# Column-halved products of key features and values in a linear-attention and feed-forward kernel

## The chip, the cores and the metric

The kernel runs on one core of one Trainium2 chip. The metric is the device time of one execution in microseconds. Before the change it is 1050.52 us, the median of three runs (1049.79 to 1050.94).

## What is computed

Attention with random features, and behind it a feed-forward layer with a gate of its own:

```
scale = 1 / sqrt(sqrt(D))                       # D = 64
def phi(x):                                     # omega: 128 features x 64
    proj = einsum('bhsd,md->bhsm', x, omega)
    h = proj - sum(x * x, axis=-1) / 2
    return exp(h - max(h, axis=-1)) / sqrt(128)
q_p, k_p = phi(q * scale), phi(k * scale)
kv  = einsum('bhsm,bhsd->bhmd', k_p, v)         # keys times values
z   = sum(k_p, axis=2)
num = einsum('bhsm,bhmd->bhsd', q_p, kv)
den = einsum('bhsm,bhm->bhs', q_p, z) + 1e-6
x   = (num / den) as 4608 tokens x 512
h   = x @ w_in                                  # 512 -> 2048
g   = h * erf(softplus(h))
out = g @ w_out                                 # 2048 -> 512
```

There are 8 batches of 8 heads, 576 positions each. Everything is in 32-bit floating point.

## The kernel before

**Tiles and stages.** Two heads make a pair: 1152 positions, cut into nine chunks of 128. There are 32 pairs. The first four are handled one by one (`first`), the others two at a time (`attention`, a quad). For each pair the key projection (`ppk`) goes through a maximum on VectorE and an exponential on ScalarE to the key features `fk`. Keys times values (`kvp`) sums over the positions: the stationary operand is a chunk of `fk`, 128 positions by 128 features, and the moving operand are the values `v`, 64 columns and a column of ones, which makes `z`. The fifth chunk holds the end of one head and the start of the other, so it is multiplied with two blocks of values at once, 130 columns, and the remaining eight with 65. VectorE or ScalarE copies `kvp` out of PSUM (`kh`, and from the thirteenth pair on a remainder `kl`). The query features are projected likewise (`ppq`), turned by transposes (`pt`), and multiplied with `kh` (`nd`); after a division they are the input `x` of the feed-forward layer. Its first product is `h`, `hS` or `hA` in the profile, its second `o`.

**The projections of a quad** (`project`, L999) put one pair's 64 dimensions in the upper and the other's in the lower 64 rows of TensorE's array, so that two products with half the rows run in one array. This is an arrangement that stands in the kernel before already.

**The order of the work.** No engine's order is written out by hand. `build` lists operations with the engines that can run them, an estimated cost (`COST`, L59) and a due time (`plan`); `Plan.order` (L135) runs through simulated time and gives each engine, when it is free, the ready operation that is due first. On TensorE it keeps account of the array's division: an operation named `proj...` has `half` set (L106), a change of `half` costs `COST["turnout"] / 2` (L246), and as long as the array is divided, another projection that is ready and due within `NEAR` = 6 us is taken ahead of a whole-array operation (L236). The order that comes out is the program order of each engine. TensorE works through it in order: a product that waits holds up all products behind it.

**What the change touches.** `key_values` of the emitter (L1017) issues `kvp` in two operations, `j` = 0 with five chunks and `j` = 1 with four; `key_values` of `build` (L575) registers them with a cost of 0.222 us a chunk and due times 0.08 of a quad's length apart, so other work can come between. `attention` (L679) calls it for both pairs of a quad, with due times 0.15 and 0.2.

The lines of the profile are those of a helper through which all instructions go (L858), so its groups are told apart by the names of the tiles.

Of the kernel before, what the change touches and what calls it, by code (L numbers as in the profile page):

```python
# [19 lines left out]
P = 128  # L20
B, H, S, D = 8, 8, 576, 64
NP = H // 2
S2 = 2 * S
NC = S2 // P
MID = NC // 2
D1 = D + 1
DM, DF = 512, 2048
T = 288
# [27 lines left out]
            ("S4", "B22", (((0, 1), (0, 1)),)))  # L56


COST = dict(mm=0.132, proj=0.224, turnout=0.40, tr=0.109, kv=0.222, table=1.3)  # L59
LAG = {"T": 0.35, "A": 0.35, "V": 0.33, "G": 0.33, "S": 0.3}  # L60
SLOTS = dict(w=8, u=2, un=2, f=2, mx=2, sq=2, v=2, qh=1, ql=1, kh=1, kl=1, rc=2, xs=4, xh=2, xl=2, u2=2,
             hs=4, gs=2, gh=6, gl=6, os=4, ps=8)
# [27 lines left out]
class Plan:  # L90
# [10 lines left out]
    def op(self, name, opts, fn, reads=(), writes=(), plan=None, set=None, macro=None, size=0,  # L101
           after=()):
        o = Op()
        o.opts, o.fn, o.plan, o.name, o.set, o.macro, o.size = opts, fn, plan, name, set, macro, size
        o.id = len(self.ops)
        o.half = name.startswith("proj")  # L106
        deps = {}
        uses = {}
        for a in after:
            deps[a.id] = a  # L110
        for t, key in reads:
            uses[t] = 1
            assert key in t.wr, (name, t.name, key)
            deps[t.wr[key].id] = t.wr[key]
            t.rd.setdefault(key, []).append(o)
        for t, key in writes:
            uses[t] = 1
            if key in t.wr:
                deps[t.wr[key].id] = t.wr[key]
            for r in t.rd.get(key, ()):  # L120
                if r is not o:
                    deps[r.id] = r
            t.wr[key], t.rd[key] = o, []
        o.alloc = []
        for t in uses:
            if not t.users:
                o.alloc.append(t)
                self.streams.setdefault(t.stream, []).append(t)
            t.users.append(o)
        o.uses = list(uses)  # L130
        o.deps = list(deps.values())
        self.ops.append(o)
        return o

    def order(self, slots, caps):  # L135
# [28 lines left out]
        ready = {e: [] for e in engines}  # L164
# [2 lines left out]
        until = {e: 0.0 for e in engines}  # L167
        events, out = [], []
        now, table, lock, bw = 0.0, "exp", None, 0.0
        port, piece, late, half = 0.0, 1.0, 0.0, False  # L170
        count = 0

        def push(o):
# [29 lines left out]
        while True:  # L203
            progress = True
            while progress:
                progress = False
                for e in engines:
                    if not idle[e]:
                        continue
                    skipped, chosen = [], None  # L210
                    while ready[e]:
                        item = heapq.heappop(ready[e])
                        o = item[2]
                        if o.start is not None:
                            continue
                        ok = can(o)
                        if ok and e == "A":
                            if lock is not None and o.set is not None and o.macro != lock:
                                ok = False
                        if ok:  # L220
                            slack = next(s for x, _, s in o.opts if x == e)
                            if e == "S":
                                ok = o.due - now < slack
                            elif o.due - now + late < slack and slack > -1e8:
                                ok = False
                        if ok:
                            chosen = o
                            break
                        skipped.append(item)
                        if len(skipped) > 500:  # L230
                            break
                    for item in skipped:
                        heapq.heappush(ready[e], item)
                    if chosen is None:
                        continue
                    if e == "T" and half and not chosen.half:  # L236
                        near = [x for x in ready[e] if x[2].half and x[2].start is None
                                and x[0] < now + NEAR and can(x[2])]
                        if near:
                            heapq.heappush(ready[e], (chosen.due, chosen.id, chosen))  # L240
                            chosen = min(near)[2]
                    o = chosen
                    progress = True
                    dur = next(c for x, c, _ in o.opts if x == e)
                    if e == "T":
                        if o.half != half:  # L246
                            dur += COST["turnout"] / 2
                        half = o.half
                        late += 0.1 * (max(0.0, now - o.due) - late)
                    if e == "V" and o.name in SHARED:  # L250

                        dur += max(0.0, until["G"] - now) % piece
                        port = now + dur
                    elif e == "G":
                        dur += max(0.0, port - now)
                        piece = dur / PIECES.get(o.name, 1) + 1e-6
                    o.eng, o.start = e, now
                    for t in o.alloc:
                        t.slot = free[t.pool].pop(0)
                        held[t.stream] += 1  # L260
                        nxt[t.stream] += 1
                    idle[e] = False
                    if e == "A":
                        if o.set is not None and o.set != table:
                            dur += COST["table"]
                            if o.set == "exp":
                                out.append("table")
                            table = o.set
                        if o.macro is not None:
                            lock = o.macro  # L270
                            if o.name.startswith("erf!"):
                                lock = None
                    out.append(o)
                    if e == "S":
                        event(now + 0.5, "idle", e)
                        begin = max(now, bw)
                        bw = begin + o.size / 300e3
                        o.end = bw + 2.0
                    else:
                        o.end = until[e] = now + dur  # L280
                        event(o.end, "idle", e)
                    busy[e] += dur
                    event(o.end, "done", o)
# [54 lines left out]
GATES0 = 10.0  # L338
RESTS0 = 15.0
SQA = 4.0  # L340
NEAR = 6.0
GROUPS = ((0, 3), (3, 6), (6, 9))
WHG = 5.0
WBG = -1e9
# [2 lines left out]
def build(emit):  # L347

    pl = Plan()
    E = emit  # L350
# [17 lines left out]
    def when(n, x):  # L368
        return pair_time(n, x) if n < NP else quad_time(n // 2, x)
# [207 lines left out]
    def key_values(n, t0):  # L577
        a = pairs[n]
        f, v = a["fk"], a["v"]
        kvp = a["kvp"] = pl.tile("ps", "kvp" + a["nm"], [P, 512], F32, "att", early(n))  # L580
        for j in range(2):
            pl.op("kv", [("T", (5 - j) * COST["kv"], -1e9)], lambda e, j=j: E.key_values(kvp, f, v, j),
                  reads=[(f, c) for c in range(NC)] + [(v, 0)], writes=[(kvp, 0)],
                  plan=when(n, t0 + 0.08 * j))
        whole = n < WHOLE
        kh = a["kh"] = pl.tile("kh", "kh" + a["nm"], [P, 2, P], F32 if whole else F32R)
        kl = a["kl"] = kh if whole else pl.tile("kl", "kl" + a["nm"], [P, 2, P], F32R)
        pl.op("kvhigh", [("V", 0.4, -1e9), ("A", 0.4, -1e9)], lambda e: E.kv_high(e, kh, kvp),
              reads=[(kvp, 0)], writes=[(kh, 0)])
        if not whole:  # L590
            pl.op("kvrest", [("V", 0.4, -1e9)], lambda e: E.kv_rest(kl, kvp, kh),
                  reads=[(kvp, 0), (kh, 0)], writes=[(kl, 0)])
# [86 lines left out]
    def attention(m):  # L679
# [2 lines left out]
        project(m, "k", 0.0)  # L682
        load(m, "q")
        key_values(2 * m, 0.15)
        key_values(2 * m + 1, 0.2)
        project(m, "q", 0.3)
        if m + 1 < N // 2:
            load(m + 1, "k")
# [152 lines left out]
def tile_attention_moe(ctx: ExitStack, tc: tile.TileContext, qT, kT, qN, kN, vP, omT, w1, w2, out):  # L841
# [64 lines left out]
    class Emit:  # L906
# [107 lines left out]
            for f, c, m, pp, k in parts:  # L1014
                act.activation(f.ap[:, c, :], pp.ap[:, k * P:(k + 1) * P], AF.Exp, bias=m)

        def key_values(self, kvp, f, v, j):  # L1017

            k = kvp.ap[:, :2 * P].rearrange("p (j d) -> p j d", j=2)[:, :, :D1]
            if j == 0:  # L1020
                pe.matmul(k, lhsT=f.ap[:, MID, :],
                          rhs=v.ap[:, MID * D1:(MID + 2) * D1].rearrange("p (j d) -> p j d", j=2),
                          start=True, stop=False)
            for c in range(MID) if j == 0 else range(MID + 1, NC):
                pe.matmul(k[:, j, :], lhsT=f.ap[:, c, :], rhs=v.ap[:, (c + j) * D1:(c + j + 1) * D1],
                          start=False, stop=c == NC - 1)


        def kv_parts(self, kvp, dst):
# [163 lines left out]
```

## Time and profile before

| | |
|---|---|
| median of the runs | 1050.52 us |
| profiled execution: time | 1049.21 us |
| profiled execution: span from the first to the last instruction | 1047.3 us |
| granted TensorE clock, mean | 0.998 |
| busy: PE, DVE, ACT, POOL | 1033.3, 757.0, 678.3, 466.9 us |
| share of the chain that ended last: PE | 93% |
| first and last start of a `kvp` matmul | 11.4 and 856.8 us |

PE is TensorE's multiplication, PEld its weight loads, DVE is VectorE, ACT is ScalarE, POOL is GpSimd. A row of a group gives the line, the engine, the operation, output<-inputs, the part of the array (rows*columns), the shape, the count, then busy time and the mean duration of one in ns, and the idle time before it with what ended it. The duration of a matmul is its way through the array; matmuls follow each other in the array like a pipeline, so their cost is read from the distances of their starts. A row of the timeline gives the start, the duration of the run of instructions that it merges, and what they are. An instruction in 32 bits on both sides has two records in the trace.

### The profile page before, as it was taken

Reading aid. Unit: us, or ns where it says so; the run is one execution under the profiler, and the core shown is the slowest. Engines: PE = TensorE matmul, PEld = TensorE weight load, DVE = VectorE, ACT = ScalarE, POOL = GpSimd, SP = SyncE. Lnnn points to the kernel's source line nnn. Section 1 sums busy time; section 2 is a strip of 40 time slices with the busy share of each in tenths; the row PEclk is TensorE's granted clock in tenths of the full one; section 3 lists DMA queues with packets and bytes.
Section 4 is the critical chain, followed back from the end, with each engine's and each line's share of the span. In section 5 each row is a group of like instructions: output and inputs, shape, how many; then the busy total and the mean of one; then the engine's idle time right before and its main releaser. Section 6 shows DMA issues by size and latency. Waiting matters only on the chain.

```text
span 1047.3 us, 21906 instructions
## 1 busy us (share of the span) xinstructions
PE 1033.3 (99%) x8208; PEld 1006.1 (96%) x8208; DVE 757.0 (72%) x1521; ACT 678.3 (65%) x1282; POOL 466.9 (45%) x469
## 2 busy tenths in 40 slices
PE   8999999999999999999999999999999999999998
PEld 7889999999999999999999999999999999999998
DVE  5989999987787577775777767776678756755541
ACT  8869958777685775766667566776567666353330
POOL 5726638867673344623455232741328212433300
PEclk9999999999999999999999999999999999999999
DMA  8664879798767787667767776677866756668771
GB/s 246 238 233 174 287 248 338 266 338 304 246 210 268 264 278 230 232 235 266 245 229 252 262 256 204 227 267 262 269 207 219 246 164 229 224 222 269 269 235 47
DMA packets 80137, 254.11 MB, mean 243 GB/s; under 512 B 8992, under 2 KB 9504, under 8 KB 80032
## 3 DMA queue, kind: packets, MB, share of 16 engines
q1 hardware_dynamic: 80032, 252.71, 71.0%
q8 instruction: 66, 1.08, 0.4%
q14 instruction: 39, 0.32, 0.1%
HBM read 218.07 MB, written 34.60 MB: 241 GB/s over the span
## 4 chain that ended last, share of the span: by engine, by line
PE 93%; DVE 2%; POOL 1%; DMA 1%; ACT 1%; SPq 1%; issue 1%; DVEq 0%; ACTq 0%
PE o L858 39%; PE hS L858 15%; PE hA L858 11%; PE h L858 9%; PE kvp L858 6%; PE nd L858 5%; PE ppq L858 3%; PE ppk L858 3%; PE pt L858 3%; DVE pw L858 1%; SPq L858 1%; DMA uq<-qT 1%; POOL unk L858 1%; ACT rc L858 0%; DVE xs L858 0%
## 5 line engine op out<-in xcount | busy, mean ns | idle before, releaser
L858 PE MATMUL o<-gh,w 128*128 128x288 f32 x2048 | 453.9, 300 | 1.9 <-DMA w<-wdw 1.4
L858 PEld LDWEIGHTS o<-gh,w 128*128 128x128 f32 x2048 | 340.4, 188 | 8.2 <-issue 1.6
L858 PE MATMUL o<-gl,w 128*128 128x288 f32 x1024 | 301.9, 295 | 0.0
L858 POOL TENSOR_TENSOR hs<-gs,hs 128x576 f32<-128x576 f32 x70 | 109.4, 1587 | 197.1 <-ACT gs L858 128.5
L858 PEld LDWEIGHTS o<-gl,w 128*128 128x128 f32 x1024 | 192.9, 188 | 0.3
L858 PE MATMUL hS<-xh,wS 128*128 128x288 f32 x768 | 186.4, 298 | 0.2 <-ACT hs L858 0.2
L858 PE MATMUL hA<-xh,w 128*128 128x288 f32 x576 | 148.3, 298 | 0.0
L858 PEld LDWEIGHTS hS<-xh,wS 128*128 128x128 f32 x768 | 134.3, 188 | 0.4 <-ACT hs L858 0.4
L858 POOL TENSOR_TENSOR gl<-hs,gh 128x576 fp32r<-128x576 f32 x64 | 99.6, 1579 | 46.7 <-ACT gh L858 29.1
L858 PE MATMUL h<-xh,w 128*128 128x288 f32 x512 | 119.5, 309 | 0.0
L858 ACT ACT_TABLE_LOAD x92 | 118.0, 1283 | 2.3 <-PEq L1184 0.7
L858 PE MATMUL hS<-xl,wS 128*128 128x288 f32 x384 | 113.3, 295 | 0.0
L858 POOL TENSOR_TENSOR unq<-unq 128x288 f32<-128x288 f32 (+2 forms) x63 | 48.1, 765 | 134.6 <-ACT unq L858 128.4
L858 ACT ACTIVATE fk<-ppk,mxk 128x128 f32<-128x128 f32 x288 | 77.4, 416 | 44.2 <-DVE mxk L858 44.0
L858 PEld LDWEIGHTS hA<-xh,w 128*128 128x128 f32 x576 | 103.3, 188 | 0.0
L858 ACT ACTIVATE rc<-nd,eps 64x288 f32<-64x288 f32 x128 | 63.5, 496 | 58.9 <-PE nd L858 55.2
L858 PEld LDWEIGHTS h<-xh,w 128*128 128x128 f32 x512 | 86.5, 190 | 2.7 <-DVE os L858 0.3
L858 ACT ACTIVATE fq<-ppq,mxq 128x128 f32<-128x128 f32 x288 | 77.9, 388 | 14.0 <-DVE mxq L858 13.8
L858 ACT ACTIVATE gs<-hs 128x1152 f32<-128x1152 f32 x64 | 73.0, 1163 | 19.8 <-DVE hs L858 19.4
L858 PE MATMUL hA<-xl,w 128*128 128x288 f32 x288 | 85.1, 296 | 0.0
L858 PE MATMUL h<-xl,w 128*128 128x288 f32 x256 | 76.1, 297 | 0.4 <-POOL xl L858 0.3
L858 PEld LDWEIGHTS hS<-xl,wS 128*128 128x128 f32 x384 | 72.4, 188 | 0.0
(109 smaller groups left out, 2100.9 us busy)
## 6 DMA issues: line engine op xcount, KB each, us to landing
w<-wdw SPq DMA_DIRECT2D x176, 512.0 KB, 4.7
wS<-wdcS SPq DMA_DIRECT2D x96, 512.0 KB, 4.8
st<-w SPq DMA_DIRECT2D x32, 512.0 KB, 4.8
wdw<-w SPq DMA_DIRECT2D x32, 512.0 KB, 3.5
w<-wdw SPq DMA_DIRECT2D x48, 256.0 KB, 4.2
v<-vP SPq DMA_DIRECT2D x32, 325.0 KB, 3.4
out<-os SPq DMA_DIRECT2D x32, 288.0 KB, 4.1
wdcS<-cS SPq DMA_DIRECT2D x16, 512.0 KB, 5.4
```

Source lines behind the costliest of these rows:

```text
L858: return tc.keep_in_program_order(method(*args, **kwargs))
```

## The change

Each chunk's product is issued as two instructions: one with the features 0 to 63 as the stationary operand, with its result in partitions 0 to 63, and one with the features 64 to 127 and partitions 64 to 127. Each stands on all 128 rows and on 64 columns of the array. The moving operand is the same for both. The two operations of a pair become one, with a cost of 1.08 us. The planner knows three divisions of the array now (`half` = 0, 1 or 2), stays in the same division when something of it is near, and `NEAR` is 12 us instead of 6. The second pair of a quad is due at 0.15 as the first, instead of 0.2. What goes in and what comes out, and the sums over chunks, are as before.

```diff
-COST = dict(mm=0.132, proj=0.224, turnout=0.40, tr=0.109, kv=0.222, table=1.3)
+COST = dict(mm=0.132, proj=0.224, turnout=0.40, tr=0.109, kv=1.08, table=1.3)
...
-        o.half = name.startswith("proj")
+        o.half = {"proj": 1, "kv": 2}.get(name[:4], 0)
...
-                    if e == "T" and half and not chosen.half:
-                        near = [x for x in ready[e] if x[2].half and x[2].start is None
+                    if e == "T" and half and chosen.half != half:
+                        near = [x for x in ready[e] if x[2].half == half and x[2].start is None
                                 and x[0] < now + NEAR and can(x[2])]
...
-NEAR = 6.0
+NEAR = 12.0
+KV1 = 0.15
...
         kvp = a["kvp"] = pl.tile("ps", "kvp" + a["nm"], [P, 512], F32, "att", early(n))
-        for j in range(2):
-            pl.op("kv", [("T", (5 - j) * COST["kv"], -1e9)], lambda e, j=j: E.key_values(kvp, f, v, j),
-                  reads=[(f, c) for c in range(NC)] + [(v, 0)], writes=[(kvp, 0)],
-                  plan=when(n, t0 + 0.08 * j))
+        pl.op("kv", [("T", COST["kv"], -1e9)], lambda e: E.key_values(kvp, f, v),
+              reads=[(f, c) for c in range(NC)] + [(v, 0)], writes=[(kvp, 0)], plan=when(n, t0))
...
         key_values(2 * m, 0.15)
-        key_values(2 * m + 1, 0.2)
+        key_values(2 * m + 1, KV1)
...
-        def key_values(self, kvp, f, v, j):
+        def key_values(self, kvp, f, v):
 
             k = kvp.ap[:, :2 * P].rearrange("p (j d) -> p j d", j=2)[:, :, :D1]
-            if j == 0:
-                pe.matmul(k, lhsT=f.ap[:, MID, :],
+            sides = (slice(0, D), slice(D, P))
+            for m in sides:
+                pe.matmul(k[m], lhsT=f.ap[:, MID, m],
                           rhs=v.ap[:, MID * D1:(MID + 2) * D1].rearrange("p (j d) -> p j d", j=2),
                           start=True, stop=False)
-            for c in range(MID) if j == 0 else range(MID + 1, NC):
-                pe.matmul(k[:, j, :], lhsT=f.ap[:, c, :], rhs=v.ap[:, (c + j) * D1:(c + j + 1) * D1],
-                          start=False, stop=c == NC - 1)
+            for c in (*range(MID), *range(MID + 1, NC)):
+                j = int(c > MID)
+                for m in sides:
+                    pe.matmul(k[m, j, :], lhsT=f.ap[:, c, m],
+                              rhs=v.ap[:, (c + j) * D1:(c + j + 1) * D1],
+                              start=False, stop=c == NC - 1)
```

More of the change, by code (lines that the diff above doesn't have):

```diff
@@ L169, in order @@
         now, table, lock, bw = 0.0, "exp", None, 0.0
-        port, piece, late, half = 0.0, 1.0, 0.0, False
+        port, piece, late, half = 0.0, 1.0, 0.0, 0
         count = 0
```

## The prediction

> **What bounds the kernel now.** I read the page first: the busy table and the chain that ended last.
>
> ```profile
> span 1047.3 us, 21906 instructions
> PE 1033.3 (99%) x8208; PEld 1006.1 (96%) x8208; DVE 757.0 (72%) x1521; ACT 678.3 (65%) x1282; POOL 466.9 (45%) x469
> ...
> PE 93%; DVE 2%; POOL 1%; DMA 1%; ACT 1%; SPq 1%; issue 1%; DVEq 0%; ACTq 0%
> PE o L858 39%; PE hS L858 15%; PE hA L858 11%; PE h L858 9%; PE kvp L858 6%; PE nd L858 5%; PE ppq L858 3%; PE ppk L858 3%; PE pt L858 3%; DVE pw L858 1%; SPq L858 1%; DMA uq<-qT 1%; POOL unk L858 1%; ACT rc L858 0%; DVE xs L858 0%
> ```
>
> TensorE carries 93% of the chain, and the next engine is busy 72% of the span. A busy share can hide waiting, because the ends of matmuls are modelled, so I asked next for the waits of PE alone; the three longest and the one of this product:
>
> ```profile
> PE ppk L858 <- ACT uk L858: 5.1, 1, 5.1
> PE o L858 <- DMA w<-wdw: 1.4, 1, 1.4
> PE ppk L858 <- DVE xs L858: 0.9, 2, 0.7
> ...
> PE kvp L858 <- DVE xs L858: 0.5, 1, 0.5
> ```
>
> Of these one, 5.1 us, is the wait for the first input; the others are about a microsecond each. So the time is the sum of what TensorE does, and a microsecond taken from it is a microsecond of the kernel, as long as nobody else becomes late.
>
> The product that changes is `kvp`. In the groups by shape each of its matmuls has two records (288 instructions, 576 records), which I call passes:
>
> ```profile
> L858 PE MATMUL kvp<-v,fk 128*128 128x65 f32 x512 | 63.5, 269 | 0.0
> L858 PE MATMUL kvp<-v,fk 128*128 128x130 f32 x64 | 12.7, 279 | 0.5 <-DVE xs L858 0.5
> ```
>
> Here 269 ns is the time that one pass is in the array, not what it costs, since passes overlap. The cost is the distance from start to start, and the timeline gives it. First the ruler, then two pieces of `kvp`, the second with the wide middle chunk (130 columns) ahead of its 65-column ones:
>
> ```profile
> 290.13 0.29 PE L858 MATMUL o<-gl,w 128*128 128x288 f32 x1
> 290.26 0.43 PE L858 MATMUL o<-gh,w 128*128 128x288 f32 x2
> 290.53 0.29 PE L858 MATMUL o<-gl,w 128*128 128x288 f32 x1
> ...
> 294.33 0.29 PE L858 MATMUL o<-gh,w 128*128 128x288 f32 x1
> 294.46 1.00 PE L858 MATMUL kvp<-v,fk 128*128 128x65 f32 x8
> 295.27 0.38 PE L858 MATMUL o<-gh,w 128*128 128x288 f32 x1
> 295.49 0.29 PE L858 MATMUL o<-gl,w 128*128 128x288 f32 x1
> ```
>
> ```profile
> 284.44 0.29 PE L858 MATMUL h<-xh,w 128*128 128x288 f32 x1
> 284.57 1.22 PE L858 MATMUL kvp<-v,fk 128*128 128x130 f32 x10
> 285.60 0.38 PE L858 MATMUL h<-xh,w 128*128 128x288 f32 x1
> 285.82 0.30 PE L858 MATMUL h<-xl,w 128*128 128x288 f32 x1
> ```
>
> Three `o` matmuls take 0.40 us, 0.133 each. From the `o` before `kvp` to the second `o` behind it 1.16 us pass (294.33 to 295.49); less two `o` at 0.133 that is 0.89 us for 8 passes, **0.111 us a pass**. The other piece: 1.38 less 0.27, 1.11 us for 10 passes, again 0.111, although two of the ten stream twice the columns. So streaming 65 columns is not what a pass waits for: what all ten share is the load of 128x128 weights, and that sets the 0.111. A pair has 18 passes, 2.0 us; 32 pairs cost 64 us, which is the 6% in the chain.
>
> **The change, part by part.** *The product.* 18 passes of 128x128 become 36 of 128x64, half of them for the left and half for the right part. No row of before has a product on half the columns. The nearest is the projection, which already runs two products at once, on the upper and the lower 64 rows:
>
> ```profile
> 296.42 0.29 PE L858 MATMUL o<-gh,w 128*128 128x288 f32 x1
> 296.64 0.37 PE L858 MATMUL ppq<-wq,uq 64*128 64x128 f32 x1
> 296.65 0.37 PE L858 MATMUL ppq<-wk,uq 64*128 64x128 f32 x1
> 296.86 0.27 PE L858 MATMUL ppq<-wq,uq 64*128 64x128 f32 x1
> 296.86 0.27 PE L858 MATMUL ppq<-wk,uq 64*128 64x128 f32 x1
> ...
> 297.97 0.27 PE L858 MATMUL ppq<-wq,uq 64*128 64x128 f32 x1
> 297.98 0.27 PE L858 MATMUL ppq<-wk,uq 64*128 64x128 f32 x1
> 298.18 0.40 PE L858 MATMUL o<-gh,w 128*128 128x288 f32 x1
> 298.42 0.30 PE L858 MATMUL o<-gl,w 128*128 128x288 f32 x1
> ```
>
> ```profile
> 296.64 0.18 PEld L858 LDWEIGHTS ppq<-wq,uq 64*128 64x128 f32 x1 [0.16 <-issue]
> 296.65 0.18 PEld L858 LDWEIGHTS ppq<-wk,uq 64*128 64x128 f32 x1
> ```
>
> Two loads and two multiplications start within 0.01 us of each other, and ten pairs of passes take 1.11 us (296.86 to 297.97): two products for the price of one. Halving the rows did not shorten a pass, still 0.111. Halving the columns should: a load of 64 columns and a stream of 65 are both half of the 128 that set 0.111, so a left-and-right pair should cost 0.056 (estimate, half of 0.111), and the wide chunk, 130 columns streamed, 0.111. A pair of heads is then 2 x 0.111 + 16 x 0.056 = 1.12 us instead of 2.0: 0.89 saved, **x 32 = -28.4 us**. Bounds of a left-and-right pair: 0.05 if it beats the halving a little (-31 us), and 0.111 if the halves share one load path or a load of half the columns takes as long as a whole one (0 us). I take 0.056, by the projection's row.
>
> The Trainium skill (TensorE: Matmul & The Clock Gate, LDWEIGHTS) has a weight load cost its number of columns over 1.2 GHz, whatever the rows: 107 ns for 128 columns, beside the 0.111 here, and the projection's unshortened pass agrees. By it the load of a half is 53 ns, and the sum would gain 1.5 us more.
>
> *Turning the array over.* The projection's rows price a change between whole and divided array: from 296.42 to 298.42 are 2.00 us; less 12 pairs of passes at 0.111 and two `o` at 0.133 there remain 0.40 us per visit, **0.20 us a switch**. Before, `kvp` needed none. The order of PE's instructions shows how many it needs now. Before, around pair 3_0 (`h` first product, `v` values, `fk` key features):
>
> ```order
> L858 MATMUL h101_1_3_3820<-xl1_1_2066,w1_1_7_52_3547 128x288
> L858 MATMUL h101_1_3_3820<-xh1_1_2029,w1_1_7_52_3547 128x288
> L858 MATMUL kvp_3_0_3841<-v_3_0_3059,fk_3_0_3682 128x2x65
> L858 MATMUL kvp_3_0_3841<-v_3_0_3059,fk_3_0_3682 128x65 x4
> L858 MATMUL h101_1_3_3820<-xh1_0_2010,w1_1_7_52_3547 128x288
> L858 MATMUL h101_1_3_3820<-xl1_0_2048,w1_1_7_52_3547 128x288
> ```
>
> Now at the same place:
>
> ```order
> L857 MATMUL h101_1_3_3935<-xl1_0_2132,w1_1_7_52_3661 128x288
> L857 MATMUL h101_1_3_3935<-xh1_0_2096,w1_1_7_52_3661 128x288
> L857 MATMUL kvp_3_0_3957<-v_3_0_3139,fk_3_0_3795 64x2x65 x2
> L857 MATMUL kvp_3_0_3957<-v_3_0_3139,fk_3_0_3795 64x65 x16
> L857 MATMUL kvp_3_1_3976<-v_3_1_3146,fk_3_1_3796 64x2x65 x2
> L857 MATMUL kvp_3_1_3976<-v_3_1_3146,fk_3_1_3796 64x65 x16
> L857 MATMUL h111_1_3_4000<-xh1_0_2096,w1_1_7_52_3661 128x288
> L857 MATMUL h111_1_3_4000<-xl1_0_2132,w1_1_7_52_3661 128x288
> ```
>
> What lay in four pieces over some 60 matmuls is one visit for both pairs. Over the program `kvp` has 18 visits: 14 with two pairs and 4 of one pair at the start. The projections keep 57 visits, and once `kvp` and a projection adjoin. I count 114 switches before and 149 now: 35 x 0.20 = **+7.0 us**. No row shows a switch to column halves; between nothing and twice the row price that is 0 to +14 us, and I take the row price, the same kind of event.
>
> *The order.* The second pair's product moves ahead by its other work: its last piece of before, the row at 294.46, started 9.9 us behind the first pair's start at 284.57, and now the whole of it stands right behind its partner. It needs the exponentials of ScalarE, and they are just in time in a visit of before:
>
> ```profile
> 283.15 2.24 ACT L858 ACTIVATE fk<-ppk,mxk 128x128 f32<-128x128 f32 x8
> ```
>
> They end at 285.39, 0.8 us behind the start of `kvp` at 284.57 (that was the partner's). Now the second pair starts 1.1 us behind the first: 0.3 us of room. With up to 0.5 us of waiting in 14 visits the bounds are 0 and +7 us; most visits have room, so I take **+1.5 us**. The query projections, which reuse the buffers that `kvp` frees, get more room. Behind a waiting `kvp` only TensorE's own products queue.
>
> *Start.* Of the 32 products 4 lie in the first 50 us:
>
> ```profile
> 0.00:50.00 50.00, 43.88 (x311) 40.01 (x311) 36.13 (x79) 42.17 (x117) 33.74 (x49) 1.00 0.76 243
> ...
> 300.00:860.00 560.00, 559.83 (x4581) 550.48 (x4580) 399.91 (x871) 369.29 (x675) 224.90 (x223) 1.00 0.71 241
> ```
>
> (The columns after the length: PE, PEld, DVE, ACT, POOL.) There PE is busy 43.88 of 50 us, and the saving nets 4 x (0.89 - 0.40) = 2 us. I let half of it be lost: **+1 us**, between 0 and +2. From 300 to 860 us, 559.83 of 560, every saving counts.
>
> *Sum.* -28.4 + 7.0 + 1.5 + 1.0 = -18.9 us. The profiled execution took 1049.2 us beside its span of 1047.3, so it would take 1030.3; the median of the runs, 1050.5, is 1.3 us above it: **1031.6 us**.
>
> **The rivals.** *The halves don't run at once, or don't get shorter (slower).* A left-and-right pair then costs 0.111, as two old halves in turn. The saving is 0, the switches stay: 1050.5 + 7.0 + 1.5 = 1059 us. For it: both halves stand on the same 128 rows, unlike the projection's, and halving the rows shortened nothing. Against: the two tiles own different columns and results. It decides from 0.092 us a pair on, where 512 x (0.111 - 0.092) no longer covers the 9.5 us of cost. Chance 13%.
>
> *Loads wait for the multiplications of the other half.* Each of the 36 passes then costs load and stream in turn, 0.056 + 0.056, and the wide ones 0.056 + 0.111: 32 x 0.111 + 4 x 0.167 = 4.2 us instead of 2.0, and 32 x 2.2 + 8.5 = +79, 1130 us. Against stand the loads of the piece at 294.46:
>
> ```profile
> L858 PEld LDWEIGHTS kvp<-v,fk 128*128 128x128 f32 x576 | 69.5, 191 | 0.7 <-DVE xs L858 0.7
> ...
> 294.33 0.99 PEld L858 LDWEIGHTS kvp<-v,fk 128*128 128x128 f32 x8
> ```
>
> Eight loads of 191 ns run from 294.33 to 295.32 beside the eight multiplications of 294.46 to 295.46, on the same rows. Chance 4%. The Trainium skill (TensorE: Matmul & The Clock Gate, Packing small matmuls) says that a load overlaps a running matmul only when the row group differs; the trace disagrees for the whole array, by the 0.111 us a pass just read, and for column halves no row of before shows it.
>
> *Partial overlap.* 0.084 a pair, midway: saving 14 us, 1050.5 - 14 + 9.5 = 1046 us. Chance 8%.
>
> *New waits.* The halves work, but each of 14 visits waits half a microsecond, and the other engines, with less time per batch, cost 3 us: -18.9 + 5.5 + 3 = 1040 us. For it: the 0.3 us of room; against: DVE at 72%. Chance 6%.
>
> **How the numbers follow.** The forecast has 69%. A measurement of this kernel can tell 0.2%, 2.1 us, from no change. Faster: 69 + 6 + 5 of partial = 80%; within: 2% of partial; slower: 13 + 4 + 1 = 18%. The forecast's own range is 1022 (free switches, no waits) to 1041 (switches at double price plus some waiting). Adding most of new waits and half of partial overlap gives 1022 to 1046, which leaves out the two slower cases and little else.
>
> **What would show it.** In the profile after, the groups of `kvp` should read 128*64, 1152 records; their starts should come in pairs 0.056 us apart from pair to pair, and a two-pair visit should take about 2.2 + 0.4 us between `h` or `o`. PE's waits should stay under 12 us in total. A pair distance near 0.11, or loads that start only when the other half has ended, would prove me wrong; so would gaps of 0.4 us at each switch, or `kvp` waiting on ACT `fk` in most visits.

## The result, and the profile after

The changed kernel takes 1036.26 us (median of 4 runs, 1033.94 to 1036.85) beside 1050.15 us before (1048.98 to 1050.94). The ratio is 0.9868, 95% interval 0.9852 to 0.9884: 13.9 us less, where 18.9 less were forecast. The page of the profile after begins:

```profile
span 1035.1 us, 23091 instructions
PE 1015.7 (98%) x8784; PEld 983.8 (95%) x8784; DVE 750.2 (72%) x1488; ACT 686.9 (66%) x1312; POOL 495.8 (48%) x479
...
PE 89%; DVE 5%; ACT 3%; issue 1%; DMA 1%; SPq 1%; POOL 0%; ACTq 0%; DVEq 0%
PE o L857 38%; PE hS L857 15%; PE hA L857 11%; PE h L857 9%; PE nd L857 4%; PE kvp L857 3%; PE ppk L857 3%; PE ppq L857 3%; PE pt L857 3%; DVE pw L857 1%; DVE xs L857 1%; DMA uq<-qT 1%; SPq L857 1%; DVE w L857 1%; ACT fq L857 1%
```

Two things moved. `kvp` has half its share of the chain, 3% instead of 6%. And PE's share of the chain fell from 93% to 89%, with VectorE at 5% and ScalarE at 3%: there are now stretches in which TensorE waits.

A visit to the column halves, with two pairs in it, reads so in the timeline:

```profile
347.31 0.29 PE L857 MATMUL hA<-xh,w 128*128 128x288 f32 x1
347.53 2.53 PE L857 MATMUL kvp<-v,fk 128*64 128x130 f32 x72
349.99 0.40 PE L857 MATMUL hS<-xh,wS 128*128 128x288 f32 x1
350.23 0.29 PE L857 MATMUL hS<-xl,wS 128*128 128x288 f32 x1
```

From 347.31 to 350.23 are 2.92 us; less two whole products at 0.133 the visit costs 2.65 us, its two turns of the array included. The forecast had 2 x 1.12 + 0.40 = 2.64. The loads of the same visit run the whole time beside the multiplications:

```profile
347.52 2.40 PEld L857 LDWEIGHTS kvp<-v,fk 128*64 128x64 f32 x72 [0.16 <-issue]
```

The waits of PE, those of half a microsecond and more:

```profile
PE ppk L857 <- ACT uk L857: 5.1, 1, 5.1
PE ppk L857 <- DVE xs L857: 2.3, 3, 1.2
PE nd L857 <- ACT qh L857: 2.2, 1, 2.2
PE kvp L857 <- ACT fq L857: 1.9, 2, 1.6
PE o L857 <- DVE w L857: 0.9, 2, 0.8
PE ppk L857 <- DVE w L857: 0.7, 1, 0.7
PE ppq L857 <- DVE xs L857: 0.6, 1, 0.6
PE pt L857 <- ACT fq L857: 0.5, 2, 0.3
```

All rows of this view add up to 15.4 us; before they added up to 10.0. The wait of 2.2 us for `qh` and that of 1.6 us for `fq` are new. Both lie at the start, where the view names 12.9 of the 15.4 us (the first 66 us; before 7.9 of 10.0), and the fourth pair shows what they do: its `kvp` starts at 46.92 us, in before at 42.78. First after, then before:

```profile
46.92 0.44 PE L857 MATMUL kvp<-v,fk 128*64 128x130 f32 x4
```

```profile
42.78 0.47 PE L858 MATMUL kvp<-v,fk 128*128 128x130 f32 x2
```

ScalarE's timeline after shows how the first of the two arises:

```profile
14.29 1.16 ACT L857 ACTIVATE uk<-uk 64x1152 f32<-64x1152 f32 x1 [0.81 <-DMA uk<-kT]
17.12 1.16 ACT L857 ACTIVATE uq<-uq 64x1152 f32<-64x1152 f32 x1 [1.67 <-DMA uq<-qT]
18.30 0.88 ACT L857 ACTIVATE fk<-ppk,mxk 128x128 f32<-128x128 f32 x3
19.06 0.50 ACT L857 ACTIVATE qh<-pt 128x384 f32<-128x384 f32 x1
```

The planner gave the square of the third pair's queries (`uq`) to ScalarE; in before it had given it to GpSimd. It waits there for its load until 17.12, and the copy of `qh`, which a product of TensorE needs, stands behind it.

Behind a wait stands another cost, which the view of waits doesn't hold. The granted clock of TensorE is 0.995 in the mean here, 0.998 before, and it isn't spread evenly. Here are two stretches in which TensorE does little, each with the stretch behind it (start and end, length, busy time and count of PE, PEld, DVE, ACT and POOL, granted clock, share of the DMA engines, GB/s):

```profile
16.00:20.00 4.00, 1.72 (x10) 0.97 (x9) 1.12 (x3) 2.86 (x8) 0.02 (x1) 1.00 1.02 390
20.00:24.00 4.00, 4.00 (x17) 3.43 (x16) 0.50 (x2) 3.83 (x11) 3.77 (x5) 0.57 1.05 392
...
54.00:58.00 4.00, 1.77 (x14) 1.33 (x14) 3.73 (x10) 1.40 (x4) 2.41 (x4) 0.99 0.57 231
58.00:62.00 4.00, 3.89 (x26) 3.69 (x27) 3.90 (x8) 3.04 (x11) 2.22 (x3) 0.50 0.00 0
```

From 20 to 24 us the clock is 0.57, where the kernel before has 1.00. From 58 to 62 us it is 0.50, where the kernel before has 0.64, and the projection's pairs of passes start 0.21 us apart (58.46, 58.67, 58.88) instead of 0.111. The first 66 us, after and then before:

```profile
0.00:66.00 66.00, 53.03 (x459) 47.49 (x461) 48.21 (x104) 50.99 (x142) 33.38 (x48) 0.92 0.67 209
```

```profile
0.00:66.00 66.00, 57.68 (x406) 51.95 (x407) 50.30 (x111) 51.11 (x142) 35.96 (x52) 0.97 0.71 232
```

By the clock alone that is 0.08 x 66 = 5.3 us beside 0.03 x 66 = 2.0, so about 3 us more (an estimate from these rows). That the waits bring the low clock is read from the order of the rows; no run tried it alone.

Two theories came out of this. **A:** the halves and the turns cost what the forecast said, and the missing 5 us are waits that the new order brings, at the start above all. **B:** the visits cost more than the two-pair visit shows, and the order is free. The runs were made on several chips; each ratio is to the kernel before on its own chip.

### The profile page after: what moved, and what is told of

The parts are those of the page before. It is cut to its first block, busy times and chain, and to the rows that moved or that the text cites. A ratio compares the mean times of both kernels' runs of the same rounds, so it can differ in the third digit from the quotient of the medians.

```text
span 1035.1 us, 23091 instructions
## 1 busy us (share of the span) xinstructions
PE 1015.7 (98%) x8784; PEld 983.8 (95%) x8784; DVE 750.2 (72%) x1488; ACT 686.9 (66%) x1312; POOL 495.8 (48%) x479
## 4 chain that ended last, share of the span: by engine, by line
PE 89%; DVE 5%; ACT 3%; issue 1%; DMA 1%; SPq 1%; POOL 0%; ACTq 0%; DVEq 0%
PE o L857 38%; PE hS L857 15%; PE hA L857 11%; PE h L857 9%; PE nd L857 4%; PE kvp L857 3%; PE ppk L857 3%; PE ppq L857 3%; PE pt L857 3%; DVE pw L857 1%; DVE xs L857 1%; DMA uq<-qT 1%; SPq L857 1%; DVE w L857 1%; ACT fq L857 1%
## 5 line engine op out<-in xcount | busy, mean ns | idle before, releaser
L857 PE MATMUL o<-gh,w 128*128 128x288 f32 x2048 | 446.2, 299 | 1.0 <-DVE w L857 0.9
L857 POOL TENSOR_TENSOR gl<-hs,gh 128x576 fp32r<-128x576 f32 x84 | 138.0, 1668 | 40.1 <-ACT gh L857 31.0
L857 POOL TENSOR_TENSOR unq<-unq 128x288 f32<-128x288 f32 (+2 forms) x63 | 50.3, 801 | 137.2 <-ACT unq L857 122.3
L857 POOL TENSOR_TENSOR unk<-unk 128x144 f32<-128x144 f32 (+2 forms) x68 | 50.5, 747 | 70.9 <-DMA unk<-kN 50.5
```

Of the source, the lines that this page charges most:

```text
L857: return tc.keep_in_program_order(method(*args, **kwargs))
```

## The experiments

**The halves alone.** The plan, the costs and every queue of before; only what a `kvp` operation issues is new:

```diff
             if j == 0:
-                pe.matmul(k, lhsT=f.ap[:, MID, :],
...
+                for m in sides:
+                    pe.matmul(k[m], lhsT=f.ap[:, MID, m],
...
             for c in range(MID) if j == 0 else range(MID + 1, NC):
-                pe.matmul(k[:, j, :], lhsT=f.ap[:, c, :], rhs=v.ap[:, (c + j) * D1:(c + j + 1) * D1],
...
+                for m in sides:
+                    pe.matmul(k[m, j, :], lhsT=f.ap[:, c, m],
...
```

> The column halves alone, in the order of before: the planner, its costs and due times are those of before, so every queue has the order of before, and each kvp product is issued as a left and a right half. The array is turned over 224 times instead of 114 (55 visits to kvp). Theory A (a left-and-right pair costs 0.056 us, a switch 0.20 us, and what the forecast missed lies in the order of the first 50 us): -28.4 + 110 x 0.20 = -6.4 us, 1044 us, with PE's waits as before. Theory B (the missing 5 us are in the visits themselves, each costing 0.28 us more than 0.40): -28.4 + 55 x 0.68 = +9 us, 1059 us.

Measured: 1042.84 us beside 1047.86, a ratio of 0.9954 (0.9934 to 0.9975), 5.0 us less. That is A's -6.4, not B's +9. PE's waits add up to 10.4 us, and the granted clock is 0.998, both as before. Its short visits also part the turn from the passes, 20 passes in the first and 16 in the second:

```profile
343.74 0.29 PE L858 MATMUL hA<-xh,w 128*128 128x288 f32 x1
343.96 0.91 PE L858 MATMUL kvp<-v,fk 128*64 128x130 f32 x20
344.80 0.40 PE L858 MATMUL hS<-xh,wS 128*128 128x288 f32 x1
345.04 0.29 PE L858 MATMUL hS<-xl,wS 128*128 128x288 f32 x1
...
350.19 0.29 PE L858 MATMUL o<-gh,w 128*128 128x288 f32 x1
350.41 0.69 PE L858 MATMUL kvp<-v,fk 128*64 128x65 f32 x16
351.03 0.40 PE L858 MATMUL o<-gh,w 128*128 128x288 f32 x1
351.27 0.29 PE L858 MATMUL o<-gl,w 128*128 128x288 f32 x1
```

Less two whole products the visits cost 1.03 and 0.81 us. The difference, 0.22, is two wide left-and-right pairs, 0.11 each. The visit of 2.65 us in the profile after has 24 narrow pairs and 4 wide ones more than the one of 0.81, so a narrow pair costs (2.65 - 0.81 - 0.44) / 24 = 0.058 us, and 0.81 - 8 x 0.058 = 0.35 us are left for the two turns. The forecast had 0.056 and 0.40.

**The order alone.** The plan and the queues of the changed kernel, with `kvp` issued whole:

```diff
-            for m in sides:
-                pe.matmul(k[m], lhsT=f.ap[:, MID, m],
...
+            pe.matmul(k, lhsT=f.ap[:, MID, :],
...
             for c in (*range(MID), *range(MID + 1, NC)):
                 j = int(c > MID)
-                for m in sides:
-                    pe.matmul(k[m, j, :], lhsT=f.ap[:, c, m],
...
+                pe.matmul(k[:, j, :], lhsT=f.ap[:, c, :], rhs=v.ap[:, (c + j) * D1:(c + j + 1) * D1],
...
```

> The order alone: the planner and every queue's order are those of the changed kernel, but kvp is issued whole, 128x128, 18 passes a pair and no column halves, so no switches for it. Theory A (the new order loses about 5 us by itself, at the start): 1036.3 + 28.4 - 7.0 = 1057.7 us, 7 us above before, with ScalarE again at the query square of the third pair at 17 us and PE waiting for qh. Theory B (the order costs nothing): 1050 us.

Measured: 1054.79 us beside 1047.86, a ratio of 1.0059 (1.0040 to 1.0078), 6.9 us more. The order alone loses time, as A says, and PE's waits add up to 15.3 us, as in the changed kernel, instead of 10.0. Of the 6.9 us the waits are 5.3; the granted clock, 0.997 beside 0.998, makes about 1 us more (an estimate: 0.003 of 1055 us beside 0.002 of 1047). The same two-pair visit, whole:

```profile
351.28 0.29 PE L857 MATMUL hA<-xh,w 128*128 128x288 f32 x1
351.42 4.13 PE L857 MATMUL kvp<-v,fk 128*128 128x130 f32 x36
355.35 0.38 PE L857 MATMUL hS<-xh,wS 128*128 128x288 f32 x1
355.57 0.30 PE L857 MATMUL hS<-xl,wS 128*128 128x288 f32 x1
```

It costs 4.29 - 0.27 = 4.02 us instead of 2.65. With the ratios 0.9868 and 1.0059 the halves in this order are worth a factor of 0.981, 20 us; the forecast's two terms for them make 21.4.

**The halves in turn.** The order of the changed kernel, but all left halves of a pair before all right ones:

```diff
             for m in sides:
                 pe.matmul(k[m], lhsT=f.ap[:, MID, m],
...
-            for c in (*range(MID), *range(MID + 1, NC)):
-                j = int(c > MID)
-                for m in sides:
+                for c in (*range(MID), *range(MID + 1, NC)):
+                    j = int(c > MID)
                     pe.matmul(k[m, j, :], lhsT=f.ap[:, c, m],
...
```

> The changed kernel with the same order of all queues, but inside a pair's kvp all left halves come first and then all right halves, so neighbouring passes use the same part of the array. If the gain comes from left and right running at once and a half's pass costs half of a whole one (0.056 us): 2 x (2 x 0.111 + 16 x 0.056) = 2.24 us a pair instead of 1.12, 32 x 1.12 = +36 us, 1072 us. If a half alone still takes 0.111 us a pass: 4.0 us a pair, +92 us, 1128 us. If the gain came from shorter passes alone, in turn: no change, 1036 us.

Measured: 1059.38 us beside 1047.86, a ratio of 1.0103 (1.0088 to 1.0119). That is 23 us above the changed kernel, which ran on another chip, and 25 us by the two ratios. Its visit:

```profile
352.07 0.29 PE L857 MATMUL hA<-xh,w 128*128 128x288 f32 x1
352.29 4.30 PE L857 MATMUL kvp<-v,fk 128*64 128x130 f32 x72
356.52 0.40 PE L857 MATMUL hS<-xh,wS 128*128 128x288 f32 x1
356.76 0.29 PE L857 MATMUL hS<-xl,wS 128*128 128x288 f32 x1
```

It costs 4.69 - 0.27 = 4.42 us, where 2 x 2.24 + 0.40 = 4.88 were worked out and the same instructions, left and right by turns, take 2.65. So a half alone costs about half of a whole pass, and two at once cost as much as one: both parts of the gain are needed. Neither a half at 0.111 (1128 us) nor a gain from shorter passes alone (1036 us) is left. The 0.46 us a visit below my sum have their place where left gives way to right: there the first pass of the right half starts (353.265 us) while three narrow ones of the left, issued earlier, are still to start (353.317 to 353.437), so some passes overlap after all. By the visits, 32 pairs lose 28 us; the time lost 23 to 25. The difference has two sources: the waits of PE fell to 12.9 us from 15.4, and the granted clock is 0.998 instead of 0.995, about 3 us less (an estimate as above).

**The square of the queries on GpSimd.**

```diff
-                  [("G", 2.2, -1e9), ("A", 1.2, -1e9)],
+                  [("G", 2.2, -1e9)] + [("A", 1.2, -1e9)] * (qk == "k"),
                   lambda e, i=i: E.pair_square(e, u, qk, i, parts),
```

> The changed kernel, in which the squares of the first pairs' queries may run on GpSimd alone (in before the planner put that of the third pair there, in the changed kernel on ScalarE, which waits for its load at 15 to 17 us with three exponentials and a copy of qh behind it). The array's divisions are counted the same, 149 switches. Theory A: the wait of 2.2 us of nd for qh goes, and with it most of the 4 us by which the start is late: 1032 us. Theory B: the start isn't it, 1036 us.

Measured: 1036.26 us beside 1047.86, a ratio of 0.9879 (0.9861 to 0.9898). No gain: this part of A is wrong. The wait for `qh` did go. That of `nd` for `mxk` grew to 1.6 us, from 0.3 in the changed kernel, and that of 1.6 us for `fq` stayed:

```profile
27.52 2.48 PE L857 MATMUL nd<-qh,kh 128*128 128x288 f32 x8 [1.62 <-DVE mxk L857]
...
33.63 1.38 PE L857 MATMUL kvp<-v,fk 128*64 128x130 f32 x36 [1.62 <-ACT fq L857]
```

The fourth `kvp` starts at 44.94 us, 2.0 us earlier than in the changed kernel. The visit at 111.57 us is 0.7 us earlier, the one at 158.82 only 0.2, and the one at 347.74 is 0.2 us later: what was won at the start was lost again. In all PE waits 16.0 us here. One operation on another engine makes the planner lay out everything behind it anew, and the new layout had its own waits.

**The start as before.** The first four pairs issue `kvp` whole, in two operations, with the costs of before, which gives the start the order of before:

```diff
+        if n < NP:
+            for j in range(2):
+                pl.op("wkv", [("T", (5 - j) * 0.222, -1e9)], lambda e, j=j: E.key_values_whole(kvp, f, v, j),
...
+                      plan=when(n, t0 + 0.08 * j))
+        else:
+            pl.op("kv", [("T", COST["kv"], -1e9)], lambda e: E.key_values(kvp, f, v),
```

> The changed kernel, but the first four pairs issue kvp as before: whole, in two operations with the costs and due times of before. The four visits of the start go, and the planner's order of the first 50 us is that of before; the projections get 59 visits instead of 57, in all 146 switches instead of 149. Theory A (the start loses the time): in before the fourth pair's kvp starts at 42.8 us, in the changed kernel at 46.9, so 4 us come back, less 4 x 0.89 - 4 x 0.4 = 2 us of saving already counted in that comparison, and 0.8 us for the two visits: 1033 us. Theory C (what is won at the start is lost again before 350 us, because another engine or the order of the middle sets the pace there): the fourth kvp is early, but the one near 348 us isn't, and the time stays at 1036 us.

Measured: 1048.26 us beside 1048.50, a ratio of 0.9991 (0.9977 to 1.0005). Neither theory had this. The fourth `kvp` starts at 43.2 us, so the start was mended; then the middle lost more than all of the gain. Its longest wait, and the stretch from 230 to 350 us (columns as in the stretches above):

```profile
PE pt L863 <- ACT fq L863: 7.0, 3, 5.5
```

```profile
230.00:350.00 120.00, 112.02 (x899) 106.35 (x901) 98.13 (x167) 80.43 (x153) 59.90 (x54) 0.96 0.73 258
```

The same stretch of the changed kernel:

```profile
230.00:350.00 120.00, 119.52 (x1057) 115.41 (x1055) 94.81 (x169) 84.56 (x173) 82.92 (x75) 1.00 0.76 271
```

TensorE gets through 899 passes instead of 1057 (they aren't all alike), is busy 7.5 us less, and has a granted clock of 0.96. The wait of 5.5 us has its chain in the timeline of the other engines:

```profile
229.90 6.57 POOL L863 TENSOR_TENSOR hs<-gs,hs 128x576 f32<-128x576 f32 x4 [0.61 <-ACT gs L863]
...
231.53 3.68 DVE L863 TENSOR_TENSOR cS<-S,cS 128x512 fp32r<-128x512 f32 x2
...
235.13 1.01 DVE L863 TENSOR_REDUCE sqq<-ppq 128x3 f32<-128x384 f32 x2
...
236.44 2.95 ACT L863 ACTIVATE fq<-ppq,mxq 128x128 f32<-128x128 f32 x11 [2.88 <-DVE mxq L863]
236.87 0.99 PE L863 MATMUL pt<-ident,fq 128*128 128x128 f32 x3 [5.47 <-ACT fq L863]
```

Two differences of weight sums hold VectorE until 235.2, the maxima of the projections come behind them, then the exponentials, then the transposes that TensorE has next in its queue. Behind the wait the clock is half:

```profile
236.80:246.00 9.20, 7.64 (x22) 5.08 (x23) 6.37 (x18) 8.36 (x27) 0.65 (x1) 0.50 0.67 249
```

So the wait of 5.5 us costs about 4 us more (an estimate, half of the 7.64 us in which TensorE is busy there).

**The same with the old due time of the second pair.** On top of the last one:

```diff
-KV1 = 0.15
+KV1 = 0.2
```

> The same as start_as_before, with the second pair's due time back at 0.2 as before the change: kvp has 18 visits instead of 14 and the projections 54 instead of 59, 144 switches instead of 146. By the switches alone 0.4 us less than start_as_before, under theory A 1033 us, under theory C 1036 us.

Measured: 1033.72 us beside 1048.50, a ratio of 0.9862 (0.9839 to 0.9884). It differs from the last kernel in one number of the planner, has two switches less, and takes 14.5 us less. PE waits 14.4 us instead of 20.1. From the changed kernel its interval doesn't part it. The profile, of an execution of 1037.18 us, above the median, shows the gain of the start kept in the middle, against C: the visit at 341.81 us stands 5.7 us ahead of the changed kernel's at 347.53. It is lost near the end, where the second product waits 3.2 us for its weights until 913.55 us and the granted clock behind it is 0.53 (915 to 920 us).

**NEAR back at 6.** In the changed kernel:

```diff
-NEAR = 12.0
+NEAR = 6.0
```

> The changed kernel with NEAR back at 6 us, all else the same. The projections then have 70 visits instead of 57, 175 switches instead of 149. With 0.20 us a switch 26 x 0.20 = +5.2 us, 1041.5 us. If switches are mostly hidden, no change, 1036 us.

Measured: 1044.82 us beside 1048.50, a ratio of 0.9962 (0.9947 to 0.9976), about 10 us above the changed kernel, where the 26 switches explain 5. PE's waits, 15.0 us, are nearly the same, and the granted clock is 0.995 to 0.997 in all runs, beside 0.995 and 0.996 in the changed kernel. The runs went from 1041.2 to 1046.4, and the profile was of the first of these; what the others did more isn't shown.

**The planner's price of `kvp`.** The start as before with `KV1 = 0.2`, and in a second kernel the changed kernel itself, each with one edit:

```diff
-COST = dict(mm=0.132, proj=0.224, turnout=0.40, tr=0.109, kv=1.08, table=1.3)
+COST = dict(mm=0.132, proj=0.224, turnout=0.40, tr=0.109, kv=1.13, table=1.3)
```

> start_as_before_kv02 with one number of the planner changed: a kvp operation is taken to cost 1.13 us, what its passes cost in the profile after, instead of 1.08. 139 switches instead of 144, the instructions are the same. If the time follows the work and the switches, 5 x 0.2 = 1 us less than start_as_before_kv02, a ratio to before of 0.985. If waits that any re-ordering brings weigh more than switches, it lands several us off that, with a wait of 2 us or more of PE in the first 350 us.

> The changed kernel with the same number, 1.13 instead of 1.08, and nothing else: the projections have 61 visits instead of 57, 158 switches instead of 149. By the switches 9 x 0.2 = +1.8 us, a ratio to before of 0.9885 where the changed kernel had 0.9868. If re-ordering by itself weighs more, it is off that by several us.

Measured: the first 1049.74 us beside 1050.20, a ratio of 1.0002 (0.9986 to 1.0019); the second 1038.71, 0.9894 (0.9874 to 0.9914). The first has the fewest switches of all kernels with column halves, 139, and gains nothing; PE waits 24.0 us, among it one of 2.9 us in the first 350 us, as the second reading of the expectation had it:

```profile
PE pt L863 <- ACT hs L863: 2.9, 1, 2.9
```

The second has 158 switches and lands where they put it, within its interval. In part that is luck: its waits are 17.3 us, 1.9 more than in the changed kernel, and its granted clock is 0.998 instead of 0.995, about 3 us less.

**Weights fetched earlier.** On top of the start as before with `KV1 = 0.2`:

```diff
-AHEAD = 40.0
+AHEAD = 48.0
```

> start_as_before_kv02 with loads of weights due 48 instead of 40 us ahead, against the wait of 3.2 us of the second product for its weights, which its profile shows. 144 switches as there. If that wait goes and nothing else moves: 1 to 3 us less, a ratio to before of 0.984; if the early loads collide with others, no gain or a loss.

Measured: 1034.10 us beside 1050.20, a ratio of 0.9857 (0.9833 to 0.9881). The wait for the weights fell from 3.2 to 0.7 us and all waits of PE from 14.4 to 11.6 in the profiles, and the clock of 0.53 behind it is gone as well; the time is not to be told from that of the changed kernel.

## Why the prediction was right, and where it was off

*The bound.* That TensorE's work is the time held where the waits were alike: the halves gave back 5 us with 10.4 us of waits beside 10.0, and 20 us with 15.4 beside 15.3. What the forecast left out is the clock at which the work is done; it took the 0.998 of before without a term for a change.

*The product.* 0.056 us for a left-and-right pair was right within the reading, 0.058, and 0.111 for a wide one too (0.11). The halves in turn show both reasons, halved passes and two at once. The slower rival (0.111 a pair, 1059 us), the partial overlap (0.084, 1046 us) and the one in which loads wait for the other half's multiplications (1130 us) are out. The rule of the Trainium skill (TensorE: Matmul & The Clock Gate, Packing small matmuls) that a load overlaps a multiplication only in another row group doesn't hold for these column halves, which stand on the same rows: 72 loads fill 2.40 us of a visit in which 72 multiplications run.

*The turns.* 0.40 us a visit by the projection's row, 0.35 by the short visits. With 14 visits of two pairs at 2.65 us and 4 of one pair at 1.12 + 0.35, `kvp` costs 43 us instead of 64: 21 us won, as the sum had it (-28.4 + 7.0).

*The order and the start.* These are the terms that were off, in size: +1.5 and +1.0 us were taken, and the order alone measured +6.9 us (ratio 1.0040 to 1.0078). The bounds that I gave, 0 to +7 and 0 to +2, held it; the value I took did not. I looked for the waits at `kvp` in the 14 visits of two pairs, by the exponentials of one visit, and there the trace has none. They came at `nd`, `ppk`, `pt` and the `kvp` of the start, behind other engines whose order the new costs had changed, and a lower clock came behind them. "PE's waits should stay under 12 us" was wrong: 15.4. The rival with new waits (1040 us) came half true: none of its half microseconds in the 14 visits, but more than its 3 us from the other engines. Theory A had the size right, and in the changed kernel the waits do lie at the start. But mending the start alone didn't settle the time: one kernel lost again by 159 us what it had won, one lost more in the middle, and one kept 5.7 us until 341 us and lost them near the end in the execution that was profiled.

*The sum.* -21.4 and +6.9 make -14.5; measured are -13.9. From waits alone, +5.4 us, it would be -16; with about +3 for the clock it is -13 (the two profiled executions differ by 12.4). The rest is within what runs of the same kernel differ by (1046.4 to 1050.2 us for the kernel before on one chip).

*Left open.* Why this planner's orders differ so much isn't settled. For one of them, the start as before, the wait is followed to VectorE's weight sums and the clock behind it. There the waits cost 10.1 us more than before and the clock about 3 (0.995 in its profile), against 28 x 0.89 - 32 x 0.20 = 18.5 us that its halves and switches should save, and still no gain was measured: some 5 us are open, and with `NEAR` back at 6 another 5. Which of the edits of the plan (one operation instead of two, its cost, `NEAR`, the due time) brings the 6.9 us of the order wasn't parted.

## What to carry to other kernels

Where a product's passes are bound by loading weights for few moving columns, splitting the stationary operand into column halves can double its rate in 32 bits, or nearly: 0.058 us a left-and-right pair instead of 0.111 a pass here, for 0.35 us per visit; gather the products so that a visit pays. When a list scheduler makes the program's order, a change of its costs is a change of its own: run the new order with the old instructions and the new instructions in the old order before you put a price on either. Small edits of costs and due times made about 15 us here with nearly the same work, as much as the change itself, so one timing of one order says little about an edit. When TensorE waits, read the granted clock behind the wait too: here about 3 us came to 5.4 us of waits.

## What was not expected of the hardware

A half of 64 columns alone costs about 0.06 us a pass, half of the 0.111 of 128 columns, with 65 columns streamed. The projection's pass stayed at 0.111 with half the rows, and I read it as a load that rows don't shorten. It doesn't show that: the projection also streams 128 columns, and the wide half passes, which load 64 columns and stream 130, cost 0.11 as well.

Behind waits of TensorE its granted clock was low for some microseconds: 0.50 from 236.8 to 246.0 us in the kernel with the start as before, behind 5.5 us of waiting, and 0.50 from 58 to 62 us in the changed kernel, behind 4 us in which it was busy for 1.77.

The two differences of 128x512 on VectorE that took 3.68 us in the kernel with the start as before lay beside GpSimd's 6.57 us of products. Two of the same shape took 1.28 us in the same trace, while GpSimd had nothing to do until 286.18 us:

```profile
284.76 1.28 DVE L863 TENSOR_TENSOR cS<-S,cS 128x512 fp32r<-128x512 f32 x2
...
286.18 1.42 POOL L863 TENSOR_TENSOR S<-R 128x256 f32<-128x256 f32 x2 [6.16 <-DVE cS L863]
```

That the two engines stood in each other's way is inferred from such rows; it wasn't tried.
